# Sliding-window attention block: two banks for the output projection's halves, a later second norm, Wo loads spread, a two-input negation, an earlier second group

## The chip, the cores and the metric

The kernel runs on one core of one Trainium2 chip. The engines are TensorE (PE in the profile, its weight loads PEld), VectorE (DVE), ScalarE (ACT), GpSimd (POOL) and SyncE (SP, which here only issues DMAs). Times are device microseconds of one launch; lower is better. Three runs of the kernel before gave a median of 1687.52 us (1686.54 to 1690.09).

## The reference

One adaLN-conditioned transformer block in fp32, S = 2048 rows, D = 576:

```python
mod = (_silu(c) @ w_mod).reshape(c.shape[0], 6, 1, -1)
sa, ca, ga, sb, cb, gb = (mod[:, i] for i in range(6))
h = _layernorm(x) * (1 + ca) + sa
x = x + ga * A(h)          # A: qkv = h @ wqkv, 32 heads of 18, causal window of 256,
                           #    softmax(q k^T * 18**-0.5) v, then @ wo
h = _layernorm(x) * (1 + cb) + sb
x = x + gb * B(h)          # B: h1 = gelu(layernorm(h) @ w1), four quarters of columns shifted
                           #    by +1, -1, +2, -2 rows, @ w2, added to h;
                           #    then h2 = gelu(layernorm(.) @ w3) @ w4 with F = 4608, added
```

The change touches the attention half and the step that joins it to the mixer: output projection (@ wo), residual add, and two layer norms.

## The kernel before

**Precision.** A product in fp32 is made of matmuls in a reduced type: each operand is split in a high and a low part, and `products()` lists the pairs that are multiplied. A contraction over 576 is four chunks of 128 rows and a tail of 64; with the split it is 14 matmuls.

**Attention.** The work is cut in 4 groups of 512 rows, and each group in 8 units of 4 heads: 32 units of some 18 us. For unit u, `scores(u)` makes the scores of each head and row tile (L511), masks them and takes the row maximum on DVE (L518), negates the maxima and splits them in a high and a low part (`mr`, L524 and L525, DVE), turns them (`mt`, L532, PE) and copies them out (`ms`, L537, ACT); a small DMA on ACT's queue (L538) writes them as two extra rows under the unit's Q, so that the second product of Q and K, in `attend(u)` (`xs`, L558 and the mask at L567), comes out with the maximum already subtracted. The exponential follows on ACT (L577, tile `P`), the product with V on PE (L588), a copy (L593, ACT), a transpose (`ot`, L599) and the division (L607, L609, DVE), and a store to `od`. One unit's scores run while the unit before is in `attend`. `pack` (L494, L497) is the set of loads, on SP's queue, that bring a unit's Q and K from DRAM. Three buffers of Q and K take turns; the third of them is a tile named `big`.

**Projections of the next group.** The Q, K and V projections of group g run between the attention matmuls of group g-1: x loads, norms, PE transposes (L381), ACT/POOL/DVE splits, 14-matmul items (L417). They are spread over a window per group, `win`, in units of time.

**Output projection.** `s4a(t)` handles row tile t, for t = 0 to 11, during the last group's units; its steps have times relative to `w1 + 0.12 + 0.72 t`, where `w1` = 22.73 is the end of the last window. Steps: load attention rows `o` and input rows `x`; transpose four chunks (`tr`, L878); copy to SBUF (`raw`, L882, ACT); high and low parts (`hi` L886, `lo` L889, POOL) into `oT`; transpose of the tail (`trt`, L893), its high part (`hit`, L896, ACT) and low part (`lot`, L899, DVE); two halves of 288 columns, each 14 matmuls in four parts (L912), each followed by the residual add (L917, DVE); the first norm (`b`: L130 statistics on DVE, root L137 and L138 on POOL, then L143 DVE and L158 ACT); modulation by two POOL operations (L925, L926); the second norm (`c`, same steps, its own root on POOL); three stores. The low part of the tail is needed by the last of the 14 products of a half only.

**Weights.** For `Wo`, a row of `ga` is loaded (L673), and five raw chunks of 288 KB (`wor`, L693) which POOL scales and ACT and DVE split. W1's chunks are loaded and split by ACT (L1008, L1009) and POOL (L1013, L1014); the last one, the tail, is loaded in tile `W14r`.

**PSUM.** Eight banks, given out by kind: scores 0 to 2 (`sc`), `xs` 3 and 4 (`st`), transposes 5 (`tr`), the product with V 6 (`av`), everything that projects 7 (`mm`). So in `s4a` the tail transpose and both halves of a tile use bank 7.

**Order.** Every step is an event with a nominal time; `play` runs them in order of time, and that fixes the order in each engine's queue:

```python
for t in range(12):
    t0 = w1 + 0.12 + 0.72 * t
    ev += [(t0 + d, f) for d, f in self.s4a(t, kp)]
```

An engine does its queue in that order, and waits by semaphores for what an instruction needs. After the attention, the mixer and the MLP (L1197 to L1468) run; the change doesn't touch them.

Of the kernel before, what the change touches and what calls it, by code (L numbers as in the profile page):

```python
# [53 lines left out]
class Kern:  # L54
# [134 lines left out]
    def phase_a(self):  # L189
# [10 lines left out]
        with ExitStack() as st:  # L200
# [14 lines left out]
            sa = kp.tile([P, KC + 1], F32, name="sa")  # L215
            ca = kp.tile([P, KC + 1], F32, name="ca")
            ones = kp.tile([P, 1], F32, name="ones")

            def clear(i):
                clear_q(i, nc.gpsimd)  # L220
# [7 lines left out]

            def consts():
                nc.gpsimd.memset(ones, 1.0)  # L230
                clear(0)
                nc.gpsimd.memset(mask, 0.0)
                nc.gpsimd.affine_select(out=mask[:, 0:P], in_=mask[:, 0:P], pattern=[[1, P]], compare_op=ALU.is_gt, fill=NEG, base=0, channel_multiplier=-1)
                nc.gpsimd.affine_select(out=mask[:, 2 * P:], in_=mask[:, 2 * P:], pattern=[[-1, P]], compare_op=ALU.is_ge, fill=NEG, base=0, channel_multiplier=1)
                nc.gpsimd.memset(maskb, 0.0)
                nc.gpsimd.affine_select(out=maskb[:, 1, :], in_=maskb[:, 1, :], pattern=[[1, P]], compare_op=ALU.is_ge, fill=NEG, base=0, channel_multiplier=-1)
                nc.gpsimd.affine_select(out=maskb[:, 0, :], in_=maskb[:, 0, :], pattern=[[-1, P]], compare_op=ALU.is_gt, fill=NEG, base=0, channel_multiplier=1)
# [262 lines left out]
            def scores(u):  # L500
# [20 lines left out]
                def neg():  # L521
                    m = box[0]
                    mr = sm.tile([P, 4, 8], F32R, tag="mr", name=f"mr{u}", bufs=2)
                    nc.vector.tensor_scalar(mr[:, :, 0:4], m, -1.0, None, op0=ALU.mult)  # L524
                    nc.vector.scalar_tensor_tensor(out=mr[:, :, 4:8], in0=m, scalar=-1.0, in1=mr[:, :, 0:4].bitcast(F32), op0=ALU.mult, op1=ALU.subtract)  # L525
                    box.append(mr)

# [159 lines left out]
            def wo_one(k, t):  # L687
                i, j = (k, KC + k) if k < KC else (2 * KC, 2 * KC + 1)

                def f():  # L690
                    Wo[k] = raw = row(f"wor{k}")[:, 0:D]
                    if k < KC:
                        nc.sync.dma_start(raw, self.wo[k * P:(k + 1) * P, :])  # L693
                    else:
                        self.load_dup(raw, self.wo[KC * P:, :])

                def scale():
                    nc.gpsimd.tensor_tensor(out=Wo[k], in0=Wo[k], in1=Wo["ga"], op=ALU.mult)

                def hi():  # L700
                    nc.scalar.copy(Wo["w"][:, i, :], Wo[k])

                def lo():
                    nc.vector.tensor_tensor(out=Wo["w"][:, j, :], in0=Wo[k], in1=Wo["w"][:, i, :].bitcast(F32), op=ALU.subtract)
                return [(t, f), (t + 0.4, scale), (t + 0.58, hi), (t + 0.64, lo)]

            order = [0, 4, 5, 1, 6, 2, 7, 3, 8]
            wt = {0: -8.975, 4: -8.955, 5: -8.954, 1: -8.7, 6: -8.69, 2: -8.68, 7: -1.5, 3: -1.2, 8: -0.9}
# [59 lines left out]
            for n, v in enumerate((2, 3, 4, 5)):  # L768
                ev += [(2.1 + 5.0 * n + d, f) for d, f in modvec(v)]
            w1 = self.win[NB - 1][1]  # L770
            ev += [(w1 - 1.7, wo_ga), (w1 - 1.15, wo_begin), (w1 + 0.03, s4_begin), (w1 + 0.4, s4_mod)]
            for k in range(KC + 1):
                ev += wo_one(k, w1 - 1.65 + 0.1 * k)
            for t in range(12):
# [79 lines left out]
        self.xnr, self.xnT, self.pg = {}, {}, {}  # L854
        self.lc = itertools.count()

    win = {1: (2.9, 9.25), 2: (9.7, 16.1), 3: (16.55, 22.73)}
    w1_d = 1.2
    o_p, o_x, o_a = 1.6, 0.42, 0.18

    def s4a(self, t, kp):
        nc, gp, Wo = self.nc, self.gp, self.Wo
        g, i = divmod(t, 4)
        box = {}
        ps = self.bank
# [23 lines left out]
            nc.gpsimd.tensor_tensor(out=box["T"][:, KC:2 * KC], in0=box["h"], in1=box["T"][:, 0:KC].bitcast(F32), op=ALU.subtract)  # L889

        def trt():
            box["q"] = ps([TAIL, P], "mm", f"oTt{t}")
            nc.tensor.transpose(box["q"], box["o"][:, KC * P:], self.ident)  # L893

        def hit():
# [5 lines left out]
        def wo(hf):  # L901
            cs = slice(hf * 288, (hf + 1) * 288)

            def part(a, b):
                def f():
                    T, W = box["T"], Wo["w"]
                    if a == 0:
                        box["po"] = ps([P, 288], "mm", f"po{t}_{hf}")
                    pl = sorted(self.products(lambda k: k, lambda k: k), key=lambda p: p[0] // KC)
                    pl = [(T[:, i, :], W[:, j, cs]) for i, j in pl]  # L910
                    for n in range(a, b):
                        nc.tensor.matmul(box["po"], pl[n][0], pl[n][1], start=(n == 0), stop=(n == len(pl) - 1))  # L912
                return f

            def add():
                x = box["x"]
                nc.vector.tensor_tensor(out=x[:, cs], in0=box["po"], in1=x[:, cs], op=ALU.add)  # L917
            return [part(a, b) for a, b in ((0, 4), (4, 8), (8, 11), (11, 14))], add

        x, y = lambda: box["x"], lambda: box["o"]  # L920
# [12 lines left out]
            st, add = wo(hf)  # L933
            e += spread(st, t0, t1) + [(t1 + 0.025, add)]
        e += [(0.86, b1), (0.88, keep(self.xp, x)), (0.89, r1), (1.06, n1), (1.13, lambda: self.norm(y(), x(), g1())), (1.19, mod)]
        e += [(1.46, keep(self.hbd, y)), (1.46, b2), (1.49, r2), (1.66, n2), (1.73, lambda: self.norm(x(), y(), g2())), (1.86, keep(self.xnd, x))]
        return e

    def s4(self, t):
# [77 lines left out]
    def load_w1(self, t0, dt):  # L1017
# [3 lines left out]
        def one(fc, t):  # L1021
# [7 lines left out]
            def more(k):  # L1029
# [1 line left out]
                    with nc.allow_non_contiguous_dma("sixteen columns of a shift group"):  # L1031
                        part(k)
                return f
            e = [(t, begin), (t + self.w1_d, hi), (t + self.w1_d + 0.05, lo)]
            return e + [(t + 0.2 * k, more(k)) for k in range(1, KC + 1) if fc == KC]
        return [e for n, fc in enumerate((KC, 0, 1, 2, 3)) for e in one(fc, t0 + dt * n)]

# [516 lines left out]
```

## Time and profile before

| | |
|---|---|
| median of three runs | 1687.52 us (1686.54 to 1690.09) |
| the profiled execution | 1684.02 us, span 1682.2 us, clock 0.996 |
| PE busy | 1644.7 us, 98% of the span |
| DVE, POOL, ACT busy | 69%, 48%, 42% |
| chain that ended last | PE 86%, DVE 5%, DMA 3%, POOL 2%, ACT 2% |

The profile takes one execution apart. "Busy" is the time in which an engine ran instructions; the chain is followed back from the last instruction to what released it. A wait is put down to the line of the waiting instruction and to what it waited for last. Windows are in microseconds from the start of the span; the attention with its projections fills it up to about 660, the mixer and the MLP the rest.

### The profile page before, as it was taken

To read this page: it belongs to the slowest core of one execution; us is meant where nothing else is said; L and a number is where in the kernel's file an instruction comes from. 1 tells how busy PE (TensorE), PEld (TensorE's weight loads), DVE (VectorE), ACT (ScalarE), POOL (GpSimd) and SP (SyncE) were. 2 spreads that over 40 slices of the span, in tenths; PEclk is the share of its full clock that TensorE was granted. 3 is DMA by queue.
4 is the path that set the end of the run, shared out by engine and by line. 5 is a ranking of instruction groups with operands and counts; after the bars stand their busy time and mean duration, and the time that the engine had idled before them with its cause. 6 is when DMAs were issued, how large, how long until landed. Compare 5 with 4: busy or idle time off the path is not lost.

```text
span 1682.2 us, 30737 instructions
## 1 busy us (share of the span) xinstructions
PE 1644.7 (98%) x11115; PEld 1425.8 (85%) x11115; DVE 1165.1 (69%) x2527; ACT 709.4 (42%) x1325; POOL 804.0 (48%) x790
## 2 busy tenths in 40 slices
PE   9999999999998999999999999999999999999999
PEld 5777888878777777888999999999999999999998
DVE  5665765665566774777788778888885666666667
ACT  3454554555455567333344343444324222222221
POOL 6432242232335552144388888888863323323335
PEclk9999999999999999999999999999999999999999
DMA  7644544543567765335465556555665454445443
GB/s 225 195 142 134 156 144 135 142 130 111 137 163 196 199 206 192 130 122 181 139 219 199 178 199 222 202 174 197 226 232 174 160 176 147 137 148 176 144 135 108
DMA packets 160767, 283.04 MB, mean 168 GB/s; under 512 B 37988, under 2 KB 77412, under 8 KB 160616
## 3 DMA queue, kind: packets, MB, share of 16 engines
q1 hardware_dynamic: 160296, 280.55, 53.6%
q8 instruction: 88, 1.44, 0.4%
q14 instruction: 63, 0.52, 0.1%
q10 hardware_dynamic: 320, 0.52, 0.1%
HBM read 168.71 MB, written 111.63 MB: 167 GB/s over the span
## 4 chain that ended last, share of the span: by engine, by line
PE 86%; DVE 5%; DMA 3%; POOL 2%; ACT 2%; issue 1%; SPq 1%; ACTq 0%; POOLq 0%; DVEq 0%
PE pall L1413 27%; PE pall L1459 24%; PE pall L417 10%; PE pall L588 4%; PE pall L558 4%; PE pall L511 4%; PE pall L567 3%; PE pall L912 2%; PE pall L834 2%; PE pall L1197 2%; DVE pall L518 1%; PE pall L599 1%; DMA wm<-in_w_mod_dram 1%; DMA Q<-ms 1%; DMA wr<-in_A_wqkv_dram 1%
## 5 line engine op out<-in xcount | busy, mean ns | idle before, releaser
L1459 PEld LDWEIGHTS pall<-W,G 128*128 128x128 f32 x3036 | 428.3, 188 | 19.2
L1459 PE MATMUL pall<-W,G 128*128 128x288 f32 x3036 | 440.6, 294 | 0.0
L518 DVE CUSTOM_DVE_ANT_0 pall<-pall,mask 128x384 f32<-128x384 f32 (+2 forms) x512 | 271.5, 543 | 189.0 <-PE pall L511 185.8
L1413 PE MATMUL pall<-LNT,W 128*128 128x512 f32 x1512 | 374.9, 390 | 0.0
L1468 DVE TENSOR_TENSOR accA<-pall,accA 128x576 f32<-128x576 f32 (+1 forms) x337 | 254.1, 756 | 120.9 <-PE pall L1459 109.2
L1384 POOL TENSOR_TENSOR g<-g,g 128x512 f32<-128x512 f32 x140 | 185.7, 1326 | 292.4 <-DVE G L1379 150.2
L1413 PEld LDWEIGHTS pall<-LNT,W 128*128 128x128 f32 x1512 | 274.8, 188 | 45.5
L577 ACT ACTIVATE P<-pall 128x512 f32<-128x512 f32 (+2 forms) x384 | 217.5, 571 | 172.8 <-PE pall L567 162.9
L1376 ACT CAST G<-g 128x512 fp32r<-128x512 f32 x249 | 151.1, 620 | 271.7 <-POOL g L1384 270.2
L1379 DVE TENSOR_TENSOR G<-g,G 128x512 fp32r<-128x512 f32 x249 | 240.6, 968 | 11.5 <-ACT G L1376 11.4
L1417 ACT ACTIVATE g<-pall 128x512 f32<-128x512 f32 x144 | 85.9, 597 | 194.4 <-PE pall L1413 184.7
L1468 DVE TENSOR_TENSOR accB<-pall,accB 128x576 f32<-128x576 f32 x134 | 101.3, 757 | 91.1 <-PE pall L1459 89.1
L417 PE MATMUL pall<-hT,Wc 128*128 128x512 f32 x504 | 160.6, 419 | 3.9 <-ACT Wc L322 1.9
L442 POOL CAST qe<-qe 128x512 fp32r<-128x512 f32 x36 | 22.7, 630 | 232.6 <-ACT qe L438 229.0
L511 PE MATMUL pall<-K,Q 108*128 108x384 f32 (+2 forms) x352 | 125.5, 367 | 2.8 <-DMA xr<-in_A_x_dram 1.8
L1413 PE MATMUL pall<-big,W 128*128 128x512 f32 x504 | 126.2, 390 | 0.0
L567 PE MATMUL pall<-maskb,identb 128*128 128x256 bf16 (+1 forms) x640 | 120.5, 254 | 0.0
L558 PE MATMUL pall<-Q,K 110*128 110x384 f32 (+1 forms) x480 | 105.9, 294 | 6.7 <-DMA Q<-ms 3.5
L1413 PEld LDWEIGHTS pall<-big,W 128*128 128x128 f32 x504 | 90.9, 188 | 14.1
L558 PEld LDWEIGHTS pall<-Q,K 110*128 110x128 f32 x480 | 86.0, 191 | 19.5 <-issue 7.5
L417 PEld LDWEIGHTS pall<-hT,Wc 128*128 128x128 f32 x504 | 87.4, 194 | 17.7 <-issue 3.3
L588 PE MATMUL pall<-P,V 128*32 128x384 f32 (+2 forms) x1408 | 84.4, 387 | 0.0
(682 smaller groups left out, 2382.5 us busy)
## 6 DMA issues: line engine op xcount, KB each, us to landing
w4d<-W SPq DMA_DIRECT2D x55, 576.0 KB
W<-w4d SPq DMA_DIRECT2D x55, 576.0 KB
w3d<-W SPq DMA_DIRECT2D x36, 640.0 KB
W<-w3d SPq DMA_DIRECT2D x36, 640.0 KB
r<-in_B_w_dram SPq DMA_DIRECT2D x36, 288.0 KB
K<-k0d SPq DMA_DIRECT2D x64, 108.0 KB
Q<-q0d SPq DMA_DIRECT2D x88, 72.0 KB
wm<-in_w_mod_dram SPq DMA_DIRECT2D x17, 288.0 KB
```

Of the source, the lines that this page charges most:

```text
L417: nc.tensor.matmul(pm, pl()[i][0], pl()[i][1], start=(i == 0), stop=(i == 13))
L511: nc.tensor.matmul(sc[:, lo:], q[0:2 * R3, h, i * P:(i + 1) * P], k[0:2 * R3, h // 2, i * P + lo:(i + 3) * P], start=True, stop=True)
L518: nc.vector.tensor_tensor_reduce(out=sc[:, lo:], in0=sc[:, lo:], in1=mask[:, lo:], scale=1.0, scalar=-3e38, op0=ALU.add, op1=ALU.max, accu ...
L558: nc.tensor.matmul(x[:, p0 * P:(p0 + w) * P], k[0:2 * R3 + 2, h // 2, (kb + 2) * P:(kb + 3) * P], q[0:2 * R3 + 2, h, q0 * P:(q0 + w) * P], ...
L567: nc.tensor.matmul(x[:, p0 * P:(p0 + w) * P], self.identb, m, start=False, stop=(n == len(ms) - 1))
L577: nc.scalar.activation(pt[:, c0:c1, h % 2, :], x[:, c0 * P:c1 * P].rearrange("p (a b) -> p a b", b=P), AF.Exp, scale=SCALE)
L588: nc.tensor.matmul(abox[0][32 * h:32 * h + 32, q0 * P:(q0 + w) * P], v[:, hh * VA:hh * VA + 32], Pt[b, h // 2][:, p0:p0 + w, h % 2, :], st ...
L1379: nc.vector.tensor_tensor(out=sp[m][:, 1], in0=src(), in1=sp[m][:, 0].bitcast(F32), op=sub)
L1384: nc.gpsimd.tensor_tensor(out=g[o] if o in g else gt(o), in0=g[a], in1=g[b], op=op)
L1413: nc.tensor.matmul(box["p"], box["l"][i][1], box["l"][i][0], start=(i == 0), stop=(i == 13))
L1459: nc.tensor.matmul(po, a, b, start=(n == 0), stop=(n == len(seq) - 1))
L1468: nc.vector.tensor_tensor(out=ac, in0=po, in1=ac, op=ALU.add)
```

## The change

1. **Banks of the output projection.** `po` is kept per half, and the tail transpose and the two halves take banks 6 (`av`) or 7 (`mm`) by a rule on nominal times: a half goes to bank 6 where its time doesn't overlap that of a unit's product with V.
2. **Second norm.** Its root goes from 1.49 to 1.62 after the tile's base, the rest by 0.08 later.
3. **Wo loads.** The five raw loads are issued from w1 - 2.7 on, 0.3 of a unit apart (before: from w1 - 1.65, 0.1 apart); the load of `ga` at w1 - 2.85 (before w1 - 1.7). Scaling and splitting stay.
4. **W1's tail.** Its split (L1008, L1009, L1013, L1014) comes 0.4 of a unit later.
5. **Negation.** The first of its two operations becomes a two-input one, with a tile of zeros, which is one more `memset` on POOL at the start.
6. **Second group.** Its window starts at 2.6 instead of 2.9 and ends where it did.

```diff
+            zeros = kp.tile([P, 4, 4], F32, name="zeros")
...
+                nc.gpsimd.memset(zeros, 0.0)
...
-                    nc.vector.tensor_scalar(mr[:, :, 0:4], m, -1.0, None, op0=ALU.mult)
+                    nc.vector.scalar_tensor_tensor(out=mr[:, :, 0:4], in0=m, scalar=-1.0, in1=zeros, op0=ALU.mult, op1=ALU.add)
...
-                return [(t, f), (t + 0.4, scale), (t + 0.58, hi), (t + 0.64, lo)]
+                return [(w1 - 2.7 + 0.3 * k, f), (t + 0.4, scale), (t + 0.58, hi), (t + 0.64, lo)]
...
-            ev += [(w1 - 1.7, wo_ga), (w1 - 1.15, wo_begin), (w1 + 0.03, s4_begin), (w1 + 0.4, s4_mod)]
+            ev += [(w1 - 2.85, wo_ga), (w1 - 1.15, wo_begin), (w1 + 0.03, s4_begin), (w1 + 0.4, s4_mod)]
...
-    win = {1: (2.9, 9.25), 2: (9.7, 16.1), 3: (16.55, 22.73)}
+    win = {1: (2.6, 9.25), 2: (9.7, 16.1), 3: (16.55, 22.73)}
...
+        base = self.win[NB - 1][1] + 0.12 + 0.72 * t
+
+        def free(a, b):
+            lo, hi = self.o_x + self.o_a - 0.08, self.o_x + self.o_a + 0.04
+            return all((base + a - n > hi) or (base + b - n < lo) for n in range(int(base), int(base) + 3))
+        if free(0.56, 0.785):
+            kinds = "mm", "av", "av" if free(0.135, 0.2) else "mm"
+        elif free(0.31, 0.53):
+            kinds = "av", "mm", "mm"
+        else:
+            kinds = "mm", "mm", "av" if free(0.135, 0.2) else "mm"
...
-            box["q"] = ps([TAIL, P], "mm", f"oTt{t}")
+            box["q"] = ps([TAIL, P], kinds[2], f"oTt{t}")
...
-                        box["po"] = ps([P, 288], "mm", f"po{t}_{hf}")
+                        box["po", hf] = ps([P, 288], kinds[hf], f"po{t}_{hf}")
...
-        e += [(1.46, keep(self.hbd, y)), (1.46, b2), (1.49, r2), (1.66, n2), (1.73, lambda: self.norm(x(), y(), g2())), (1.86, keep(self.xnd, x))]
+        e += [(1.46, keep(self.hbd, y)), (1.46, b2), (1.62, r2), (1.74, n2), (1.81, lambda: self.norm(x(), y(), g2())), (1.94, keep(self.xnd, x))]
...
-            e = [(t, begin), (t + self.w1_d, hi), (t + self.w1_d + 0.05, lo)]
+            d = self.w1_d + 0.4 * (fc == KC)
+            e = [(t, begin), (t + d, hi), (t + d + 0.05, lo)]
```

The rule of point 1 gives these banks:

| tile | first half | second half | tail transpose |
|---|---|---|---|
| 0, 7, 11 | 6 | 7 | 7 |
| 1, 2, 4, 6, 8 | 7 | 6 | 6 |
| 5, 9 | 7 | 6 | 7 |
| 3, 10 | 7 | 7 | 6 |

Before, all were 7. The changed code has its lines 2 further down from L524 on and 13 further down in `s4a` (the projection's matmul is L925, the tail transpose L906).

Where the Wo loads stand in SP's queue: before, the last of a unit's Q and K stores, then `ga` and the four first `wor` chunks in a row, with a load of modulation weights `wm` between, then the pack of a unit into `big`:

```order
L623 DMA od_131<-o_4996 128x4x72
L454 DMA q0d_143<-qe_2_4999 128x512
L454 DMA q1d_144<-qe_2_4999 128x512
L673 DMA ga<-modd_133 128x576
L693 DMA wor_5057<-in_A_wo_dram 128x576
L642 DMA wm_4238<-in_w_mod_dram 64x576
L693 DMA wor_5077<-in_A_wo_dram 128x576
L693 DMA wor_5088<-in_A_wo_dram 128x576
L693 DMA wor_5109<-in_A_wo_dram 128x576
L494 DMA big<-q0d_141 18x2x512
```

After, `ga` and the first two chunks stand one unit earlier, round a full `wm` load that was there alone, and ahead of the pack into the second Q buffer:

```order
L460 DMA k0d_151<-qe_6_4787 128x512
L460 DMA k1d_152<-qe_6_4787 128x512
L625 DMA od_131<-o_4795 128x4x72
L675 DMA ga<-modd_133 128x576
L695 DMA wor_4846<-in_A_wo_dram 128x576
L644 DMA wm_4240<-in_w_mod_dram 128x576
L695 DMA wor_4897<-in_A_wo_dram 128x576
L496 DMA Q_171<-q0d_141 18x2x512
```

The other three chunks follow one by one, with the loads of a pack between them.

POOL's queue at tiles 0 and 1, before (`b0rs` and `c0rs` are the roots of tile 0's first and second norm, `or` and `s4rows` the rows that are modulated):

```order
L925 TENSOR_TENSOR or_5318<-or_5318,cb 128x576
L926 TENSOR_TENSOR or_5318<-or_5318,sb 128x576
L137 TENSOR_SCALAR c0rs<-c0mv 128x1
L138 TENSOR_TENSOR c0rs<-c0rs,mhalf 128x1
L886 CAST oT_5791<-oh_5778 128x512
L889 TENSOR_TENSOR oT_5791<-oh_5778,oT_5791 128x512
L137 TENSOR_SCALAR b1rs<-b1mv 128x1
L138 TENSOR_TENSOR b1rs<-b1rs,mhalf 128x1
L925 TENSOR_TENSOR s4rows<-s4rows,cb 128x576
```

and after:

```order
L938 TENSOR_TENSOR or_5320<-or_5320,cb 128x576
L939 TENSOR_TENSOR or_5320<-or_5320,sb 128x576
L899 CAST oT_5790<-oh_5780 128x512
L902 TENSOR_TENSOR oT_5790<-oh_5780,oT_5790 128x512
L137 TENSOR_SCALAR b1rs<-b1mv 128x1
L138 TENSOR_TENSOR b1rs<-b1rs,mhalf 128x1
L137 TENSOR_SCALAR c0rs<-c0mv 128x1
L138 TENSOR_TENSOR c0rs<-c0rs,mhalf 128x1
L938 TENSOR_TENSOR s4rows<-s4rows,cb 128x576
```

The root of the second norm now stands behind tile 2's high and low part and behind tile 1's first root, and directly ahead of tile 1's modulation.

PE's queue in unit 2, before the second `xs` on `big`, before (`x` are rows of the second group that are transposed, `identb` with `maskb` the mask):

```order
L558 MATMUL pall<-Q_171,K_173 128x256
L567 LDWEIGHTS identb
L567 MATMUL pall<-maskb,identb 128x128
L511 MATMUL pall<-K_172,Q_170 128x256
L558 MATMUL pall<-big 128x384
L558 MATMUL pall<-big 128x128
```

and after:

```order
L560 MATMUL pall<-Q_171,K_173 128x256
L569 LDWEIGHTS identb
L569 MATMUL pall<-maskb,identb 128x128
L513 MATMUL pall<-K_172,Q_170 128x256
L383 MATMUL pall<-ident,x_793 128x128
L383 MATMUL pall<-ident,x_817 128x128
L383 MATMUL pall<-ident,x_836 128x128
L383 MATMUL pall<-ident,x_856 128x128
L560 MATMUL pall<-big 128x384
L560 MATMUL pall<-big 128x128
```

Four of the twenty transposes of the second group's first rows stand there now, and twelve more ahead of these, between the unit's `mt` and its first `xs` on `big`.

More of the change, by code (lines that the diff above doesn't have):

```diff
@@ L911, in f @@
                     for n in range(a, b):
-                        nc.tensor.matmul(box["po"], pl[n][0], pl[n][1], start=(n == 0), stop=(n == len(pl) - 1))
+                        nc.tensor.matmul(box["po", hf], pl[n][0], pl[n][1], start=(n == 0), stop=(n == len(pl) - 1))
                 return f
@@ L916, in add @@
                 x = box["x"]
-                nc.vector.tensor_tensor(out=x[:, cs], in0=box["po"], in1=x[:, cs], op=ALU.add)
+                nc.vector.tensor_tensor(out=x[:, cs], in0=box["po", hf], in1=x[:, cs], op=ALU.add)
             return [part(a, b) for a, b in ((0, 4), (4, 8), (8, 11), (11, 14))], add
```

## The prediction

> **What bounds the kernel now.** I read the page first, then the table by stage, then PE's waits in each stage that the change touches, then single places in order of time.
>
> ```profile
> span 1682.2 us, 30737 instructions
> PE 1644.7 (98%) x11115; PEld 1425.8 (85%) x11115; DVE 1165.1 (69%) x2527; ACT 709.4 (42%) x1325; POOL 804.0 (48%) x790
> ...
> 430.00:470.00 40.00, 36.50 (x289) 29.07 (x286) 23.33 (x74) 19.15 (x35) 15.25 (x13) 0.96 0.53 143
> 470.00:660.00 190.00, 176.50 (x1564) 146.16 (x1564) 127.71 (x446) 113.83 (x208) 90.92 (x112) 0.99 0.68 188
> 830.00:1682.00 852.00, 848.80 (x5010) 771.55 (x5008) 622.83 (x779) 292.12 (x537) 505.95 (x415) 1.00 0.53 178
> ```
>
> The lower rows are a stretch, its length, and the busy time of PE, PEld, DVE, ACT and POOL, then clock, DMA share and GB/s. PE is full: it is idle 37.5 us of 1682. From 830 on 3.2 us are idle in 852, and the change doesn't reach there, so what it wins before is kept. No edit takes a matmul away. The gain can only come from idle PE time in the first 660 us, and a third of all idle time (13.5 us) lies in the 190 us of the output projection:
>
> ```profile
> PE pall L558 <- ACT P L577: 2.5, 3, 1.5
> PE pall L912 <- DVE oT L899: 2.0, 5, 0.6
> PE pall L511 <- DMA xr<-in_A_x_dram: 1.8, 1, 1.8
> PE pall L893 <- DVE s4rows L917: 1.7, 4, 0.5
> PE pall L912 <- DVE s4rows L917: 1.5, 3, 0.8
> PE pall L912 <- POOL b2rs L138: 1.0, 1, 1.0
> PE pall L878 <- DVE o L609: 0.8, 1, 0.8
> PE pall L912 <- DVE xr L917: 0.5, 1, 0.5
> ```
>
> These are PE's waits from 470 to 660: the waiting line, what ended the wait, the sum, how often, the longest.
>
> **1. Banks.** A projection half (L912) that waits for the tail's low part (L899) needs that part only in its last product; at its first matmul it waits because tail and half share bank 7. The tail transposes (L893) and halves that wait for the residual add (L917) wait for the same bank. The wait put down to POOL's root is of this kind too: a first half of tile 3, whose operand POOL had finished before. Together 2.0 + 1.7 + 1.5 + 0.5 + 1.0 = 6.7 us. By the table of banks each of these 14 waits, taken by its tile, has its neighbour in the other bank now, so all 6.7 go. Bank 6 brings a new one: a half or a tail there waits for ACT's copy of a unit's output, and the unit's first product with V waits for the add. No row shows that. The bounds: nothing, if the nominal times hold, and 6.7 if every wait returns in the other bank with its old length. I take none here and book returns below.
>
> **2. W1's tail.**
>
> ```profile
> PE pall L558 <- ACT P L577: 1.5, 1, 1.5
> ...
> ACT W L1009 <- DMA W14r<-in_B_w_dram: 1.8, 1, 1.8
> ```
>
> These are PE's waits from 515 to 522 and ACT's from 514 to 519. ACT stands 1.8 us at the split for W14r's load; the exponentials are queued behind it, and PE waits 1.5 us for one. The split 0.4 unit (7 us) later finds its load landed. Gain 1.5 (0 if another wait of ACT stands there, 1.5 at most). Its POOL part is not waited for at that place.
>
> **3. Wo loads.**
>
> ```profile
> 414.52 0.57 SPq L642 DMA_DIRECT2D wm<-in_w_mod_dram  x1
> ...
> 417.43 0.65 ACTq L538 DMA_DIRECT2D big<-ms  x1
> ...
> 420.29 0.40 PE L558 MATMUL pall<-big 110*128 110x384 f32 x2
> ...
> 432.81 0.38 SPq L673 DMA_DIRECT2D ga<-modd  x1
> ...
> 435.73 0.62 ACTq L538 DMA_DIRECT2D Q<-ms  x1
> ...
> 441.93 0.41 PE L558 MATMUL pall<-Q,K 110*128 110x384 f32 x1 [3.19 <-DMA Q<-ms]
> ```
>
> Times are start and length; the last row's bracket is the idle time before it. At 441.93 PE has waited 3.2 us for the maxima of unit 21, whose 16 KB were issued at 435.73.
>
> ```profile
> DMA packets 639, 1.31 MB, mean 218 GB/s; under 512 B 71, under 2 KB 71, under 8 KB 639
> wor<-in_A_wo_dram SPq DMA_DIRECT2D x3, 288.0 KB
> ...
> q1 hardware_dynamic: 509, 1.03, 102.2%
> ...
> q10 hardware_dynamic: 10, 0.02, 4.4%
> ```
>
> The first two rows are the DMAs from 434 to 440; the third is the only queue with packets from 436 to 440; the last is from 440 to 441. SP's loads (q1) fill the engines, and the small DMA's packets (q10) come when they are through. So the wait is the loads' time: from 432.81 to 441.93 are 9.1 us; ga, four chunks and half a `wm` are 5.5 loads of 288 KB, 1.62 MB, at 218 GB/s 7.4 us, and 1.7 remain for issue and landing. After, ga and two chunks stand a unit earlier round a whole `wm`: four loads, 5.4 + 1.7 = 7.1 us. Counted from the place of that `wm`, 414.52, they are through at 421.6, and PE wants unit 20's maxima at 420.29: a new wait of 1.3. The other three chunks come singly, between loads of packs of 72 and 108 KB, and make no wait. Net 3.2 - 1.3 = 1.9, between 0 (the new wait as long as the old) and 3.2 (none).
>
> [...]
>
> **4. Second group sooner.**
>
> ```profile
> PE pall L381 <- DVE o L609: 0.9, 1, 0.9
> PE pall L558 <- ACT P L577: 0.9, 1, 0.9
> PE pall L558 <- DMA big<-ms: 0.8, 1, 0.8
> ...
> L381 PE MATMUL pall<-ident,x 128*128 128x128 f32 (+1 forms) x20 | 3.0, 273 | 0.9 <-DVE o L609 0.9
> ...
> PE pall L558 <- ACT P L577: 0.5, 1, 0.5
> ...
> PE pall L381 <- ACT ms L537: 0.7, 1, 0.7
> PE pall L532 <- DVE mr L525: 0.3, 1, 0.3
> ```
>
> The first four rows are from 90 to 104, where the second group's transposes begin; the next from 205 to 216, the last two from 335 to 346, the same place of groups three and four. PE waits 2.6 us at the first. The window opens 0.3 unit sooner, 16 of the 20 transposes (20 take 3.0 us busy, so 2.4 us) move between the unit's `mt` and its first `xs` on `big`; that covers the 0.8 for the maxima's DMA, and the other two waits lose their neighbours. The two later groups pay 0.5 and 1.0, mean 0.75, at an undisturbed place, and I take that as what is left: 2.6 - 0.75 = 1.8. Ends: 2.6, and -1.0, if the transposes wait for `ms` in the transposes' bank as in group four and nothing else goes. On SP the group's loads pass one pack; they are issued earlier than needed.
>
> **5. Second norm.**
>
> ```profile
> L137 POOL TENSOR_SCALAR c0rs<-c0mv x1: 223/223/223, 501.3 to 501.3; 128x1 f32<-128x1 f32 x1
> L138 POOL TENSOR_TENSOR c0rs<-c0rs,mhalf x1: 567/567/567, 501.6 to 501.6; 128x1 f32<-128x1 f32 x1
> ...
> DVE pall L518 <- PE pall L511: 39.5, 41, 3.8
> DVE c11rs L143 <- POOL c11rs L138: 1.0, 1, 1.0
> ```
>
> The root (0.22 + 0.57 = 0.8 us) now stands directly ahead of the next tile's modulation on POOL, and behind two other tiles' steps. Whoever waits is DVE at L143, and behind it the row maxima that PE needs. At worst 12 tiles x 0.8 = 9.5 us. But DVE itself waits 39.5 us for PE's scores from 470 to 660, 41 times, a us each, and for a root only once, 1.0 us at the last tile. Most of the 0.8 lies in that slack; I take -1.0, the one such wait once more, with ends 0 and -9.5. In return POOL's parts for tile t+2 come 0.8 sooner; that is not on PE's path once the bank is free, and I count nothing.
>
> **6. Negation, zeros.**
>
> ```profile
> L524 DVE TENSOR_SCALAR mr<-m x32: 171/175/1124, 56.1 to 634.4; 128x16 fp32r<-128x16 f32 x32
> L525 DVE SCALAR_TENSOR_TENSOR mr<-m,mr x32: 174/176/1281, 56.3 to 634.7; 128x16 fp32r<-128x16 f32 x32
> 556.28 1.45 POOL L926 TENSOR_TENSOR s4rows<-s4rows,sb 128x576 f32<-128x576 f32 x1
> 556.48 1.28 DVE L525 SCALAR_TENSOR_TENSOR mr<-m,mr 128x16 fp32r<-128x16 f32 x1
> ```
>
> Both forms take 175 ns (the middle figure) and both have stood behind POOL: the two-input one ended with POOL's operation at 557.7. So the form changes nothing: 0, with ends of 0.5 either way, the 0.2 (470 to 660) and 0.3 that PE waits at L532. The memset of 16 elements is bounded by L137's 0.22 us, ahead of all work that waits.
>
> **Sum.** 6.7 + 1.5 + 1.9 + 1.8 - 1.0 + 0 = 10.9 us. What is late next: with 8.2 us of idle time out of the output projection, PE meets exponentials (the remaining 1.0 of 2.5), POOL's parts of `oT` and the attention rows (0.8) sooner, with DVE at 67% and ACT at 60%. I let a quarter return, 2.0 (ends 0 and 8.2; nearest to the rows that remain, 1.8). Net 8.9: 1684.02 - 8.9 = 1675.1 for the profiled execution. The median stands 3.5 above it, so 1678.6.
>
> **Rivals.**
> - *All of it comes.* Nothing returns, no new wait at unit 20, no root on the path: 6.7 + 1.5 + 3.2 + 2.6 = 14.0, 1673.5. For it: the idle time of DVE. Against: groups three and four, which still wait.
> [...]
> - *The waits come back.* Bank 6's copy and add, POOL's parts and the exponentials take all of term 1. What stays is 1.5 and half of 1.9 + 1.8, 3.3: 1684.2, which is no change. For it: DVE, ACT and POOL are at half load or more in this stretch, and each wait is 0.5 us, short enough to be replaced.
> - *Slower: the roots hold DVE.* DVE stands at L143 for c(t) while POOL does the next modulation's last operation (1.45) and the root (0.8): 2.25 per tile, 27 over 12, 1687.5 - 9.9 + 27 = 1704.6. It decides from (9.9 + 3.4) / 12 = 1.1 us per tile that reaches PE. Against it: the slack of a us that DVE has 41 times.
>
> **How the numbers follow.** About 0.2%, 3.4 us, is what can be told from no change. Chances: forecast 0.57 (its own range 1675 to 1683), all of it 0.13, the small DMA 0.06, waits back 0.15, roots 0.09. Faster 0.57 + 0.13 + 0.06 = 0.76, same 0.15, slower 0.09. The range goes from all of it less 2 us (single runs lay 1.0 below and 2.6 above their median), 1671.5, to the waits back with the 3.5 between profiled execution and median once more, 1688.0; outside are the roots and a tail on the low side.
>
> **What would show it.** Right: from 470 to 660 no wait of L925 for L912, and PE busy about 96% of that stretch (176.5 of 190 - 8.2 + 2.0); no wait of ACT at L1022 for W14r; no wait of some 3 us for `ms` of unit 21, and about 1.3 of unit 20's; the three waits between 90 and 104 gone but for 0.8. Wrong: L925 or the product with V waiting for the add in bank 6; PE's scores waiting for row maxima with DVE at L143 before; transposes that wait for `ms`; unit 20 waiting as long as 21 did.

## The result, and the profile after

The changed kernel takes 1677.69 us (median of 4, 1677.1 to 1679.28) against 1687.03 us (median of 4 at that time), a ratio of 0.9944 with a 95% interval of 0.9927 to 0.9961: 9.3 us less. The profiled execution took 1678.03 us, span 1676.2.

The page of the kernel after, its span and the row of busy times:

```profile
span 1676.2 us, 30727 instructions
PE 1639.8 (98%) x11115; PEld 1423.4 (85%) x11115; DVE 1170.9 (70%) x2527; ACT 707.6 (42%) x1325; POOL 806.1 (48%) x791
```

Two stretches of its table by stage (stretch, length, busy time of PE, PEld, DVE, ACT, POOL, clock, DMA share, GB/s):

```profile
430.00:470.00 40.00, 39.54 (x321) 32.17 (x319) 26.92 (x86) 22.20 (x40) 17.23 (x15) 1.00 0.48 133
470.00:660.00 190.00, 177.67 (x1575) 148.12 (x1574) 129.49 (x447) 114.35 (x211) 89.73 (x110) 0.99 0.70 191
```

The first stretch is full now (39.5 of 40 us, before 36.5, and the clock 1.00 in place of 0.96). The second is hardly fuller: PE is idle 12.3 us in it, before 13.5 (the window now holds some 6 us more of what follows). What it waits for is another list. PE's waits from 470 to 660, kernel after (line, what ended it, sum, times, longest):

```profile
PE pall L513 <- DMA hbd<-s4rows: 3.6, 1, 3.6
PE pall L560 <- ACT P L579: 1.8, 3, 1.1
PE pall L534 <- DVE mr L527: 1.4, 3, 0.6
PE pall L513 <- DMA k0d<-qe: 1.1, 1, 1.1
...
PE pall L590 <- DVE oT L912: 0.6, 1, 0.6
PE pall L906 <- DVE s4rows L930: 0.3, 1, 0.3
```

No wait of the projection's matmul (L925) is left, and of the 6.7 us for the shared bank 0.9 came back (the last two rows). But the first scores of unit 27 (L513) stand 3.6 us for that unit's Q and K (the row names a store, `hbd`, that SP issues behind those loads; the matmul reads only the unit's K and Q), and the turned maxima (L534) and an exponential (L560) cost some 1.1 us each at places where nothing waited before (1.4 in place of 0.2 us for the first; 1.1 of the 1.8 for the second).

**Half clock.** Behind some waits the granted clock is 0.50 for 3.4 us. The two such places of the kernel before (after its first 40 us), and then the one of the kernel after, as rows of the table by stage:

```profile
442.63:446.05 3.42, 3.42 (x15) 2.44 (x17) 1.76 (x6) 1.18 (x2) 3.42 (x4) 0.50 0.59 144
521.14:524.55 3.41, 3.41 (x17) 3.22 (x17) 1.74 (x8) 2.25 (x4) 0.95 (x1) 0.50 0.87 296
```

```profile
529.89:533.31 3.42, 3.15 (x13) 3.09 (x14) 1.04 (x4) 1.68 (x3) 0.00 (x0) 0.50 1.03 313
```

At a clock of 0.50 I count half of the 3.4 as lost, an estimate: 1.7 us on top of the wait ahead of it. PE counts as busy in it (3.42, 3.41 and 3.15 us in the rows). The first stands behind the wait for unit 21's maxima (441.93), the second behind 1.5 us for an exponential and 1.0 us at tile 3's first half, the third behind the new wait for Q and K.

**Where the time went, by marks.** The start of the transposes of the maxima (L532 before, L534 after) marks each unit in every trace. The table gives the time of a stretch less that of the same stretch in the first profile of the kernel before: up to unit 0, units 0 to 10 (second group), 20 to 22 (Wo loads), 22 to 31 (output projection), from 31 to PE's end, and the whole (units 10 to 20, within 0.4 us in all of these rows, only in the whole); then the time at half clock after the first 40 us.

| profile | to 0 | 0-10 | 20-22 | 22-31 | 31-end | whole | half clock |
|---|---|---|---|---|---|---|---|
| before, second profile | +1.5 | +2.5 | +0.5 | -0.3 | +0.8 | +5.2 | 17.1 |
| after | -1.1 | +0.1 | -3.2 | -2.1 | +0.2 | -6.0 | 3.4 |
| banks alone | +1.1 | +0.1 | +0.6 | -3.3 | +0.6 | -0.8 | 6.8 |
| Wo loads alone | +0.5 | +0.2 | -1.0 | +1.2 | +1.1 | +2.0 | 10.2 |
| second group alone | +1.1 | -0.3 | -1.4 | +0.2 | +1.0 | +0.8 | 3.4 |
| after, old roots | -0.4 | -1.0 | -1.6 | -5.0 | +0.2 | -7.4 | 6.8 |
| after, old W1 tail | -0.2 | -0.1 | -3.1 | -0.2 | +0.1 | -3.4 | 6.8 |
| after, old negation | +0.1 | -0.3 | -3.3 | -0.7 | 0.0 | -4.0 | 6.8 |
| after, Wo behind a pack | +2.1 | -0.3 | -4.7 | -1.2 | -0.3 | -4.2 | 6.8 |
| that and old roots | +1.6 | +0.1 | -4.9 | -6.9 | +0.5 | -9.5 | 3.4 |

A profile is one execution, and the first profile of the kernel before was a short one (1684.02; 29 runs of it beside the first experiments had a median of 1686.99). The stretch up to unit 0, which no edit touches but for one `memset`, alone moves between -1.1 and +2.1 us from profile to profile. So medians with intervals carry the verdicts here, and marks only say where.

### The profile page after: what moved, and what is told of

Same layout as the page of the kernel before. It is cut to its first block, busy times and chain, and to the rows that moved or that the text cites. A ratio compares the mean times of both kernels' runs of the same rounds, so it can differ in the third digit from the quotient of the medians.

```text
span 1676.2 us, 30727 instructions
## 1 busy us (share of the span) xinstructions
PE 1639.8 (98%) x11115; PEld 1423.4 (85%) x11115; DVE 1170.9 (70%) x2527; ACT 707.6 (42%) x1325; POOL 806.1 (48%) x791
## 4 chain that ended last, share of the span: by engine, by line
PE 84%; DVE 5%; DMA 4%; POOL 2%; ACT 2%; issue 1%; SPq 1%; ACTq 0%; POOLq 0%; DVEq 0%
PE pall L1427 27%; PE pall L1473 24%; PE pall L419 9%; PE pall L590 4%; PE pall L560 4%; PE pall L513 4%; PE pall L569 3%; PE pall L836 2%; PE pall L925 2%; PE pall L1211 2%; DVE pall L520 1%; PE pall L601 1%; DMA wm<-in_w_mod_dram 1%; DMA big<-ms 0%; DMA wr<-in_A_wqkv_dram 0%
## 5 line engine op out<-in xcount | busy, mean ns | idle before, releaser
L513 PE MATMUL pall<-K,Q 108*128 108x384 f32 (+2 forms) x352 | 125.6, 368 | 6.0 <-DMA hbd<-s4rows 3.6
L560 PE MATMUL pall<-Q,K 110*128 110x384 f32 (+1 forms) x480 | 105.5, 293 | 2.6 <-ACT P L579 1.5
L560 PEld LDWEIGHTS pall<-Q,K 110*128 110x128 f32 x480 | 85.4, 190 | 15.7 <-issue 4.8
```

Source lines behind the costliest of these rows:

```text
L513: nc.tensor.matmul(sc[:, lo:], q[0:2 * R3, h, i * P:(i + 1) * P], k[0:2 * R3, h // 2, i * P + lo:(i + 3) * P], start=True, stop=True)
L560: nc.tensor.matmul(x[:, p0 * P:(p0 + w) * P], k[0:2 * R3 + 2, h // 2, (kb + 2) * P:(kb + 3) * P], q[0:2 * R3 + 2, h, q0 * P:(q0 + w) * P], ...
```

## The experiments

### The kernel before, once more

No edit.

> The kernel before once more, unchanged, for a second profile of it. The waits of PE between 40 and 660 come out as in the first, each within 0.3 us, except the one at unit 21 (3.2 us in the first, 3.4 and 3.8 in the profiles with that place unchanged), and the stretches of half clock differ in number or length, by 3.4 us each, 1.7 us lost for each: the time lies up to 3.4 us from the first profile's 1684.0.

It took 1689.2 us. Most waits came out as expected (between 90 and 107: 0.9, 0.9 and 0.8 again); five were off by 0.3 or more, the largest by 0.7 (Q and K at 481, 1.1 in place of 1.8). It had five windows of half clock after the first 40 us, 17.1 us, 8.5 lost, where the first profile had 6.8 and 3.4. The stretches, kernel before, second profile:

```profile
58.33:61.74 3.41, 3.41 (x14) 2.78 (x12) 0.84 (x6) 0.57 (x1) 0.00 (x0) 0.50 0.96 315
95.88:99.29 3.41, 3.41 (x17) 3.07 (x15) 1.70 (x5) 2.10 (x4) 0.61 (x1) 0.50 0.50 152
447.45:450.86 3.41, 3.41 (x14) 2.19 (x17) 1.77 (x6) 1.05 (x2) 3.41 (x3) 0.50 0.58 120
522.54:529.37 6.83, 6.25 (x26) 5.60 (x27) 2.68 (x12) 4.06 (x8) 3.50 (x6) 0.50 0.81 221
```

The 5.2 us between the two spans are these 5.1 us and 1.5 at the start, less 1.4 for what else differs. The time differed by more than the 3.4 us expected, by the mechanism that was expected.

### One part alone

The kernel before with one part of the change each.

```diff
-            box["q"] = ps([TAIL, P], "mm", f"oTt{t}")
+            box["q"] = ps([TAIL, P], kinds[2], f"oTt{t}")
-                        box["po"] = ps([P, 288], "mm", f"po{t}_{hf}")
+                        box["po", hf] = ps([P, 288], kinds[hf], f"po{t}_{hf}")
```

> The kernel before with part 1 alone (banks). Theory (waits moved): the 14 waits for the shared bank, 6.7 us, go, and with the 2.9 us of them that lie between 515 and 521 the dip of the granted clock behind them (0.77 and 0.81 from 519 to 527, some 1.7 us); but part of it returns as a wait for the Q and K loads of unit 27, as in the changed kernel (3.6 us and a dip there). Here W1's tail still holds PE 1.5 us, so that wait is about 2 us. Net 3 to 5 us: 1682 to 1684 on a median of 1687. Rival (the sum as predicted): no new wait, 6.7 to 8.4 us, 1678.6 to 1680.3. A second rival (the banks are no gain, all returns): 1686 to 1688.

1682.81 us, ratio 0.9977 (0.9969 to 0.9986): 3.9 us, 2.4 to 5.2. The theory's 3 to 5. PE's waits from 470 to 660 in it:

```profile
PE pall L558 <- ACT P L577: 3.0, 4, 1.7
PE pall L532 <- DVE mr L525: 1.7, 2, 1.1
PE pall L511 <- DMA W12r<-in_B_w_dram: 1.7, 1, 1.7
...
PE pall L588 <- DVE oT L910: 0.6, 1, 0.6
...
PE pall L904 <- DVE s4rows L928: 0.3, 1, 0.3
```

The bank's waits are gone but for the same 0.9, and with no other part of the change the wait for unit 27's loads is there (the third row). So the banks' part alone is enough to bring that wait.

```diff
-                return [(t, f), (t + 0.4, scale), (t + 0.58, hi), (t + 0.64, lo)]
+                return [(w1 - 2.7 + 0.3 * k, f), (t + 0.4, scale), (t + 0.58, hi), (t + 0.64, lo)]
-            ev += [(w1 - 1.7, wo_ga), ...
+            ev += [(w1 - 2.85, wo_ga), ...
```

> The kernel before with part 3 alone (Wo loads). Theory A (wait and clock): the 3.2 us wait for unit 21's maxima goes and with it the dip of the clock behind it (0.83 and 0.74 from 440 to 448, 0.17 x 4 + 0.26 x 4 = 1.7 us), a wait of 1.5 us comes at unit 20: gain 3.4 us, 1683.6 on 1687. At unit 22 the maxima's transposes stand 3 to 3.5 us earlier than before. Theory B (the wait alone, as predicted): 3.2 - 1.3 = 1.9 us, 1685.1. Theory C (the loads are not the cause): the 3.2 us wait stays, 1687.

1685.83 us, ratio 0.9992 (0.998 to 1.0004): 1.3 us, not to be told from none. The 3.2 us at unit 21 are gone, as with every other kernel that has this part, but here the new wait at unit 20 was longer and had a half clock behind it. PE's wait from 418 to 440, and the row of the table by stage behind it:

```profile
PE pall L558 <- DMA big<-ms: 2.2, 1, 2.2
```

```profile
424.02:427.44 3.42, 3.42 (x13) 2.84 (x12) 1.25 (x4) 1.19 (x2) 2.16 (x2) 0.50 0.44 90
```

In the six other profiles that have this part as it is, that wait is 1.3 to 1.8 us, and one of them (1.6 us) has the half clock behind it. Theory C is out; A's 3.4 is at the edge of the interval and B's 1.9 well inside it, so the sizes stay open.

```diff
-    win = {1: (2.9, 9.25), 2: (9.7, 16.1), 3: (16.55, 22.73)}
+    win = {1: (2.6, 9.25), 2: (9.7, 16.1), 3: (16.55, 22.73)}
```

> The kernel before with part 6 alone (second group sooner). Theory (waits moved, as the marks of the changed kernel say): the three waits between 90 and 104 go, 2.6 us, and new ones of the same sum come, at the first transposes (0.75), at the next (0.96) and at the maxima (0.54): gain 0 +- 0.5 us at unit 10, 1687. Prediction: 1.8 us, 1685.2.

1685.14 us, ratio 0.9991 (0.9983 to 1.0): 1.5 us, 0 to 2.9. The profile says that the waits only changed names. PE's waits from 86 to 112 in it, in the place of 0.9, 0.9 and 0.8:

```profile
PE pall L381 <- ACT h L389: 1.0, 1, 1.0
PE pall L381 <- ACT ms L537: 0.8, 1, 0.8
PE pall L532 <- DVE mr L525: 0.5, 1, 0.5
```

By marks units 0 to 10 gained 0.3 us, in the other profiles with this part between 1.0 gained and 0.1 lost. The half clock at 95.88 of the second profile of the kernel before, behind two of the old waits that stand 1.5 us apart, comes in none of the 10 profiles with this part; in the four without it, it came once. That may be the rest of the 1.5, but one case in four doesn't settle it.

### One part undone

```diff
-        e += [(1.46, keep(self.hbd, y)), (1.46, b2), (1.62, r2), (1.74, n2), ... (1.94, keep(self.xnd, x))]
+        e += [(1.46, keep(self.hbd, y)), (1.46, b2), (1.49, r2), (1.66, n2), ... (1.86, keep(self.xnd, x))]
```

> The changed kernel with part 2 undone (second norm's root where it was). If the later roots cost what was predicted: 1.0 us less, 1676.7 on 1677.7. If DVE's slack hides them: no change within 0.5 us, 1677.7. If the roots' place is what frees POOL for the next tile's parts: slower by up to 2 us, 1679.7, with PE waiting for POOL's parts of oT.

1676.65 us, ratio to before 0.9942 (0.9928 to 0.9956), 1.0 us less than the changed kernel. The interval doesn't tell it from the changed kernel, and with the Wo loads moved (below), where the same edit takes 3.2 us off the median, the single runs overlap; the profile shows where the late roots cost something. POOL of the kernel after at the second norm of tile 5 (start, length, operation):

```profile
571.48 0.22 POOL L137 TENSOR_SCALAR b6rs<-b6mv 128x1 f32<-128x1 f32 x1 [1.30 <-DVE b6mv L132]
571.79 0.56 POOL L138 TENSOR_TENSOR b6rs<-b6rs,mhalf 128x1 f32<-128x1 f32 x1
572.34 0.21 POOL L137 TENSOR_SCALAR c5rs<-c5mv 128x1 f32<-128x1 f32 x1
572.63 0.57 POOL L138 TENSOR_TENSOR c5rs<-c5rs,mhalf 128x1 f32<-128x1 f32 x1
```

ACT's wait at that place (from 570 to 578), and then PE's row in order of time:

```profile
ACT s4rows L158 <- DVE c5rs L143: 1.8, 1, 1.8
```

```profile
576.80 0.52 PE L560 MATMUL pall<-Q,K 110*128 110x384 f32 x2 [1.09 <-ACT P L579]
```

The root of tile 5's second norm stands behind the root of tile 6's first; ACT stands 1.8 us at the normalisation (L158) that needs it, unit 27's exponentials are queued behind, and PE waits 1.09 us. That wait, 1.09 us, is in all six profiles with the late roots and in none of the eight with the old ones. But it isn't the whole price: in the profiles with the new banks and the old roots, PE stands some 0.5 us longer for the turned maxima just ahead of that place. From 550 to 580 its waits add up to 2.1 us here (1.1 at L534, 1.0 at L513) and to 2.7 in the changed kernel (1.1 at L560, 0.6 at L534, 0.5 at L513 and two shorter ones), so in waits of PE the late roots cost 0.6 us there.

```diff
-            d = self.w1_d + 0.4 * (fc == KC)
+            d = self.w1_d
```

> The changed kernel with part 4 undone (W1's tail split where it was). ACT waits 1 to 2 us for W14r again and PE 1.0 to 1.7 us for an exponential. If this adds as predicted: 1677.7 + 1.5 = 1679.2, with a half clock behind it 1680.9. If PE then only waits less for unit 27's loads (3.6 us at 530): no change, 1677.7 +- 0.5.

1678.47 us, ratio 0.995 (0.9937 to 0.9964): 0.8 more than the changed kernel, inside the interval. PE waits 2.1 us for exponentials (1.6 and 0.5, with 6.8 us of half clock behind the first), and then none of the 3.6 for unit 27's Q and K; the 0.4 us at that place are for a row maximum of DVE. The first rows of its waits from 510 to 540:

```profile
PE pall L560 <- ACT P L579: 2.1, 2, 1.6
PE pall L513 <- DVE m L520: 0.4, 1, 0.4
```

So the two waits stand for each other: PE comes later to unit 27, by the exponentials and the half clock, and finds its loads there.

```diff
-                    nc.vector.scalar_tensor_tensor(out=mr[:, :, 0:4], in0=m, scalar=-1.0, in1=zeros, op0=ALU.mult, op1=ALU.add)
+                    nc.vector.tensor_scalar(mr[:, :, 0:4], m, -1.0, None, op0=ALU.mult)
```

> The changed kernel with part 5 undone (first negation a one-input operation). As predicted: no change, 1677.7 +- 0.5, and the first of the two operations has the same lengths unit by unit (499 and 494 ns, 481 and 481 ns in the two profiles so far at units 7 and 16). If the two-input form were the slower one beside POOL: 0.5 us or more less here, with the long ones shorter.

1678.67 us, ratio 0.9952 (0.9937 to 0.9966): no difference to be told. Its first negation, and behind it that of the changed kernel (minimum, middle and longest of 32, in ns):

```profile
L524 DVE TENSOR_SCALAR mr<-m x32: 168/175/1277, 56.6 to 630.4; 128x16 fp32r<-128x16 f32 x32
```

```profile
L526 DVE SCALAR_TENSOR_TENSOR mr<-m,zeros x32: 174/176/1290, 55.1 to 628.2; 128x16 fp32r<-128x16 f32 x32
```

The form changes nothing that these runs can tell.

### The new wait for unit 27's Q and K

SP's queue in the kernel after, from the stores of the output projection to the first of unit 27's loads:

```profile
510.79 0.54 SPq L942 DMA_DIRECT2D xnd<-xr  x1
...
511.90 0.65 SPq L942 DMA_DIRECT2D hbd<-s4rows  x1
512.61 0.45 SPq L1009 DMA_DIRECT2D W11r<-in_B_w_dram  x1
...
514.55 0.58 SPq L882 DMA_DIRECT2D s4rows<-od  x1
...
516.18 0.34 SPq L496 DMA_DIRECT2D Q<-q0d  x1
```

The buffer is free at 513.97 (PE's last matmul on it) and the loads are issued from 516.18 on. Their packets run from 518.5 to 528.8, and the scores that wait for them start at 530.16.

```diff
-        e = [(-0.6, load_o), (-0.35, load_x)]
+        e = [(-0.6 + 0.33 * (t == 4), load_o), (-0.35 + 0.09 * (t == 4), load_x)]
-        ... (0.88, keep(self.xp, x)) ... (1.46, keep(self.hbd, y)) ...
+        ... (0.88 + 0.27 * (t == 2), keep(self.xp, x)) ... (1.46 + 0.42 * (t == 1), keep(self.hbd, y)) ...
-        return [e for n, fc in enumerate((KC, 0, 1, 2, 3)) for e in one(fc, t0 + dt * n)]
+        return [e for n, fc in enumerate((KC, 0, 1, 2, 3)) for e in one(fc, t0 + dt * n + 0.4 * (n == 2))]
```

> The changed kernel, with five steps that stand ahead of unit 27's Q and K loads on SP's queue (one store of the first norm's rows, a W1 chunk, a store and two loads of the output projection) put behind them. Theory A (the loads are late because SP's queue and its transfers come first): the first of them is issued 2.2 us sooner, 514 in place of 516.2, and has no rows of 288 KB ahead; the wait of 3.6 us at 530 shrinks to under 1 us and the half clock behind it (3.4 us long, 1.7 us lost) goes: 1677.7 - 2.6 to 4.3 = 1673.4 to 1675.1. Theory B (the loads themselves take some 12 us whatever stands ahead): the wait shrinks by no more than 1 us, 1676.7 to 1677.7. Theory C (what is put behind is now late): the wait moves to the attention rows of tile 4 at the transposes of the output projection, 1677.7 or more.

1681.68 us, ratio 0.997 (0.9959 to 0.9981): 4 us worse than the changed kernel. Theory C: the loads begin at 513.58 and nobody waits for them. Their packets run from 514.5 to 524.7, as long as in the changed kernel (10 us), so it is their start that moved. But tile 4's attention rows are late, and 6.8 us of half clock follow. PE's only wait from 520 to 540:

```profile
PE pall L891 <- DMA s4rows<-od: 4.7, 1, 4.7
```

The same without `load_o` moved:

```diff
+        e = [(-0.6, load_o), (-0.35 + 0.09 * (t == 4), load_x)]
```

> The changed kernel with two stores, a W1 chunk and one load (four of the five steps of the last try, without the load of tile 4's attention rows) put behind unit 27's Q and K loads. If those loads are late because of what stands ahead: the wait of 3.1 to 4.1 us at 530 shrinks to 1 or 2 us, the half clock behind it goes, and no new wait for tile 4's rows comes: 1677.7 - 2 to 4 = 1673.7 to 1675.7. If another thing ends last (the attention rows again, or the loads' own time): a wait of 3 us or more stays in that place, 1677 to 1682.

1678.46 us, ratio 0.9954 (0.9939 to 0.9968). In the profile the wait for the loads is gone (0.4 us for a row maximum are left at that place), the stretch 22 to 31 is 4.2 us shorter than before (2.1 in the changed kernel) and no half clock is left after the first 40 us, so what stands ahead of the loads does make them late. Yet its span, 1676.1, is that of the changed kernel, 1676.2: a wait of 0.9 us comes at unit 28, and the stretch up to unit 0, ahead of all that the edit touches, took 2.2 us more in this execution. The median doesn't gain either. What takes it back in other executions, one profile doesn't show: open.

### The Wo loads, elsewhere

```diff
-                return [(w1 - 2.7 + 0.3 * k, f), (t + 0.4, scale), (t + 0.58, hi), (t + 0.64, lo)]
+                return [(w1 - 2.1 + 0.03 * k, f), (t + 0.4, scale), (t + 0.58, hi), (t + 0.64, lo)]
-            ev += [(w1 - 2.85, wo_ga), ...
+            ev += [(w1 - 2.15, wo_ga), ...
```

> The changed kernel with ga and all Wo chunks issued in a row behind the Q and K loads of unit 22, half a unit ahead of the maxima of unit 21. If the waits at units 20 and 21 are made by the Wo loads that stand ahead of the small DMA: both are under 0.5 us now, and the 1.5 to 2.2 us at unit 20 with the half clock that follows in two of three profiles go: 1677.7 - 1.5 to 3.2 = 1674.5 to 1676.2. If the loads slow unit 22's Q and K: a wait at its first scores of 1 to 3 us, 1677 to 1680. If the loads are not the cause, the wait at unit 20 stays as it is, 1677.7.

1677.71 us, ratio 0.9944 (0.9926 to 0.9962): no gain in the median (single runs from 1672.9 to 1682.4). In the profile, however, both waits are gone, that at unit 20 and that at unit 21: PE waits for nothing between 415 and 450. So the loads ahead of the small DMA make them; units 20 to 22 are 4.7 us shorter than before. The packets of the small DMA say the same. In the kernel before, the first of them comes 1.3 us after the issue at units 17 to 20 and 4.5 us after it at unit 21, behind the loads; in the changed kernel it comes after 2.9 us at unit 20; here after 1.3 us at unit 20 and 1.75 at unit 21. Why the median doesn't gain stays open. In the profiled execution the wait for unit 27's Q and K is still 3.1 us, and the stretch up to unit 0, which the edit doesn't touch, is 3.2 us longer than in the profile of the changed kernel.

> The changed kernel with the second norm's root back at its place and the Wo chunks behind unit 22's loads: the two edits that each left a wait shorter. If they add: 1677.7 - 1.0 - 1.5 = 1675.2 (half clocks may add or take 1.7). If the waits of the Q and K loads of unit 27 take back what is won ahead of it: 1676.7.

This is the same edit with the old roots: 1674.51 us (1673.95 to 1675.63), ratio 0.9927 (0.9914 to 0.9941). It has the lowest median of all, 3.2 us under the changed kernel, and its five runs lie below all four of that kernel. The same kernel with late roots has a median 3.2 higher, but its runs scatter around these. The wait for unit 27's loads is 1.5 us and the wait for an exponential at 577 is gone; the longest of PE's waits from 524 to 536:

```profile
PE pall L513 <- DMA W12r<-in_B_w_dram: 1.5, 1, 1.5
```

With the old roots one store of 288 KB (`xnd` of tile 0) stands a few places earlier on SP, which may be why; that was not tried alone.

> root_wo and stores_behind together. If the three add: 1672 to 1674. If stores_behind moves its wait as the larger try did: 1677 or more.

1676.64 us, ratio 0.9943 (0.9927 to 0.996): the three don't add. The wait for unit 27's loads is gone, and unit 28's scores get one instead, with a half clock behind it:

```profile
PE pall L513 <- DMA s4rows<-od: 2.2, 1, 2.2
```

## Why the prediction was right, and where its steps were not

The time was forecast at 1678.6 and came at 1677.69, inside the range and on the right side. That it came within a microsecond is luck: the gain was added up from waits of PE alone, and a good part of what came is clock, which the prediction left out.

For the profiled execution the sum gave 1675.1, and it took 1678.03: by the profiles the gain is 6.0 us and not 8.9, and of these 6.0 half clock makes 3.4 (13.7 us of it before and 6.8 after, the first 40 us counted in). And the 3.5 us that I added for "the median stands above it" did not apply: the changed kernel's profiled execution stands 0.3 above its median. The second profile of the kernel before has 5.1 us more lost at half clock than the first, so the first was a short execution, and the 3.5 no constant of the kernel.

By the medians the gain is 9.3 us (6.6 to 12.3). An estimate of its two parts takes (1 - granted clock) x span of each run as lost: 8.5 us on average over the 53 runs of the kernel before that were timed beside the experiments, 4.2 over the four of the changed kernel. The clock of a run is recorded to 0.001, which is 1.7 us, so this is rough; it leaves about 4 us of the gain to the clock and about 5 to the waits, for which the sum had 8.9.

Alone or undone, the six parts come to 3.9 (banks), -1.0 (second norm), 1.3 (Wo loads), 0.8 (W1's tail), 1.0 (negation) and 1.5 us (second group), together 7.5. Only the first is clear of noise, so the runs don't show whether the parts add.

- **Banks (6.7).** Right in mechanism: 0.9 of the 6.7 are left, and bank 6 brought only those. Alone worth 3.9 us (2.4 to 5.2).
- **What is late next (2.0 of 8.2).** The term that failed. By marks the output projection gave 2.1 us in place of 8.2 - 2.0 - 1.0 = 5.2. I listed exponentials, POOL's parts and the attention rows as what comes next; the largest was none of them but the Q and K loads of unit 27 behind SP's stores and weight loads: 3.6 us, and 1.7 for the half clock behind it (the kernel before lost as much to one of its own in this stretch). PE was to be busy about 96% of the stretch from 470 to 660, and is 93.5% (177.67 of 190 us).
- **W1's tail (1.5).** ACT's 1.8 and PE's 1.5 are gone; worth 0.8 by the median, which isn't clear of noise: without this part the wait for unit 27's loads vanishes.
- **Wo loads (3.2 - 1.3 = 1.9).** Right: the 3.2 went, the new wait was 1.5 in the profile after and 1.3 to 2.2 in others. That the loads are the cause is shown by the kernel with all of them behind a pack, where both waits are gone. The 0.06 of the chances stood for a small DMA that the loads don't hold up; that is out: in the kernel before, its first packet came 4.5 us after the issue at unit 21, behind the loads, and 1.3 us after it at units 17 to 20. Alone the part is worth 1.3 us, not clear of noise. Left out was the clock: 1.7 us with either wait, when it comes.
- **Second group (1.8).** Too large. The three old waits went and 2.3 us of new ones came, among them the one that I had as the lower end, transposes that wait for the maxima's copy. 0.3 us by the profile alone, 1.5 (0 to 2.9) by the median.
- **Second norm (-1.0).** The sign agrees, but isn't clear of noise: undoing it took 1.0 off the median and, beside the moved Wo loads, 3.2; PE's waits from 550 to 580 make it 0.6. I looked at DVE and its slack; it was ACT that stood at the instruction after it (L158), with exponentials behind it.
- **Negation, zeros (0).** Right.
- **Range.** Its upper end, 1684.2 + 3.5, is 1687.7 and not 1688.0; nothing hangs on it.
- **Rivals.** "The waits come back" came half true for term 1, and "the roots hold" named a cost that is there at no more than about a tenth of the 27 us, by way of another engine.

## What to carry to other kernels

When PE is full and short waits are removed, the sum of the waits is not what comes: here 6.7 us alone were worth 3.9, and PE stood 1.7 us of the rest at loads whose place in SP's queue had not moved with it. For each wait removed, look on every queue, the one that issues DMAs first, for what PE will reach sooner, and how much slack it has. Waits of 1.6 to 4.7 us had half clock behind them here, though not each, by estimate 1.7 us more for each 3.41 us at a clock of 0.50, and taking such a wait away can win them (last section). For an operation that is moved later, look at each engine that stands in line for its result, and what is queued behind on that engine.

## What the runs showed of the hardware

I had not expected that a wait of 1.6 to 4.7 us can cost another 1.7 (the estimate above). In the profiles before and after, the clock is recorded as 0.50 or 1.00, and the halved stretches after the first 40 us are 3.41 us long; in the second profile of the kernel before one is 6.83. They follow waits of PE, but not each: the wait at unit 21 had one behind it at 3.2 and 3.7 (the two profiles of the kernel before) and 3.8 us (banks alone) and none at 3.4 (second group alone); that at unit 20 had one at 2.2 (Wo loads alone) and, of three at 1.6, behind one (old roots), and none at 1.3, 1.5 (the kernel after) and 1.8. Since they come or don't from execution to execution, they make much of the scatter of the times (5.1 of the 5.2 us between the two profiles of the kernel before), 1.7 us a step, which is more than most parts of this change are worth. Among the 53 runs of the kernel before, the 20 at a granted clock of 0.996 have a median of 1685.22 us, the five at 0.993 one of 1689.66.

The halved stretches of one profile start whole multiples of 3.413 us apart: 521.14 - 442.63 is 23 of them in the first profile of the kernel before, 522.54 - 447.45 is 22 and 447.45 - 58.33 is 114 in the second. From one execution to the other they don't (447.45 - 442.63 is 4.82). With the first 40 us left out, I divided the profiles before and after into stretches of that length and place, up to PE's end. Three of these at full clock have a halved one behind them, and in these three PE is idle 2.71, 2.07 and 3.32 us. In the other ones at full clock it is idle for 1.48 us at most, and none has a halved one behind it. The three, two of the kernel before and one of the kernel after (the stretch, its length, PE's busy time, and behind the engines the clock):

```profile
439.22:442.63 3.41, 0.70 (x6) 0.69 (x7) 0.18 (x2) 0.01 (x1) 3.33 (x3) 1.00 0.94 233
517.73:521.14 3.41, 1.34 (x8) 1.07 (x9) 1.15 (x7) 2.45 (x6) 2.71 (x5) 1.00 0.93 227
```

```profile
526.48:529.89 3.41, 0.09 (x1) 0.00 (x0) 2.87 (x13) 0.45 (x1) 1.55 (x4) 1.00 1.04 222
```

The first of them holds most of the wait at unit 21. In "second group alone" the 3.4 us of that wait lie over two such stretches, with PE idle for 1.82 us in one and 1.53 in the other, and neither has a halved one behind it:

```profile
438.12:441.54 3.42, 1.60 (x12) 1.28 (x10) 1.25 (x4) 1.52 (x3) 1.31 (x1) 1.00 1.03 293
441.54:444.95 3.41, 1.88 (x13) 1.74 (x14) 1.01 (x4) 1.02 (x2) 3.33 (x4) 1.00 0.74 146
```

So where a wait lies may matter beside its length, but these rows don't settle it: with the old roots PE is idle for 1.65 us from 416 to 424, less than the 1.82 above, and the clock is 0.75 from 420 to 424 and 0.82 from 424 to 428. What decides there these runs don't show.
